# Second channel product with the weights stationary and 256 tokens moving, its results transposed in place

## The chip, the cores and the metric

The kernel runs on one core of a Trainium2 chip. The metric is device microseconds of one execution: three runs of the kernel before took 783.22, 783.54 and 783.66 us.

## The reference

Two blocks, all in float32. The first is a linear attention for 8 batches, 8 heads, 576 tokens and a head size of 64: `kv = k^T v` per head, `out = q kv`, divided by its root mean square over the head and multiplied by `g_norm`. Its result, as x with 8 x 576 rows of 512 columns, goes through an MLP mixer:

```
h  = relu(x^T w_tok1) w_tok2        # over the tokens: 576 -> 256 -> 576
u  = x + h^T
h2 = relu(u w_ch1) w_ch2            # over the columns: 512 -> 1536 -> 512
out = u + h2
```

The change concerns the last product, `relu(u w_ch1) w_ch2`, and how its result is added to u in `out`.

## The kernel before

**Stages.** Up to 188 us attention and token mixing run in four passes of two batches each, with the channel weights loaded beside them. Their order is written out by hand as lists of step names (`start`, `middle`, `steady`, `last`; lines 1242 to 1263 and 1302). The rows of u are written to `out` (the last 64 rows of each batch also to a tensor `u_rest`). The channel mixing then works on 9 "units" of 512 rows: the first 512 rows of each batch, and as ninth unit the 8 x 64 rows that are left. Unit 0 is a group of its own (`channel1_once`, `channel2_once`, 188 to 261 us); groups 1 to 4 are units (1, 2), (3, 4), (5, 6), (7, 8), each some 129 us: first channel product, then second.

**The products.** Each channel product is cut by Strassen's scheme twice: seven outer products `o`, each made of seven inner products `p`, so 49 per channel product and group. One inner product is one "place" in the order of the program: `products[place]` holds it, and `beside[place]` the steps of the other engines that are put behind it (`put`, line 858; they are issued place by place in the loop at line 1364). Products of neighbouring `o` overlap (`PLACE`, line 854): the last inner product of one stands at its place 9, behind the second of the next. An inner product of the first channel is 3 matmuls with 256 tokens moving (line 973); of the second, two halves of 128 tokens by 3 matmuls, with the activations stationary and 128 columns of weights moving (line 1028). Float32 matmuls are two records each in the trace. Results gather in three PSUM tiles `a`, `b` (one buffer each) and `d` (two). `outer` (line 861) moves them out: ScalarE copies some, VectorE adds others (`join`, line 921, at places 5 and 6 of an outer product), and a PSUM tile can only be used again after that. Into the second channel's results `r` (128 partitions by 4 x 256, tags `us` with three buffers and `r` with three) they go as rows of tokens.

**VectorE's own work beside it** are the sums that the inner products need as operands: `ins` (line 1080) for the second channel, `inner_u` for the first, with the sums of activations `S1` to `S4`, all at fixed places (lines 1106 to 1115). It also transposes the u of the next group in blocks of 32 x 32 (`turn_tile`, line 615), which SP sends to DRAM and fetches back (`put_blocks`, `fetch_half`).

**Weights and queues.** The parts of both weights lie in DRAM and are fetched for every outer product in four transfers, 12, 9, 7 and 4 places ahead (`fetch_ahead`, line 955), into two buffers each. SP issues nearly all transfers, in order. POOL issues the accumulating ones: `join` (line 1118) adds a finished `r` to the rows of u in `out`, one DMA of 128 x 4 x 1 KB per tile for units 1 to 7, two for unit 8. In the last group the half of the columns that is finished last isn't accumulated by DMA: u is loaded as `xg` (`fetch_x`, line 597), VectorE adds to it, and `store_rest` and `store_part` (lines 1163 and 1167) write it. The second weights are loaded by `get_ch2` (line 222), six blocks of 1 MB as pairs of 32-bit words, two DMAs each; `decode` turns them into float32 on ScalarE and VectorE. Parts of that weight's tile serve as scratch for early transposes of u (`turn_early`), so the decode of some blocks waits until SP's stores of these have landed.

Of the kernel before, what the change touches and what calls it, by code (L numbers as in the profile page):

```python
# [11 lines left out]
F32 = mybir.dt.float32  # L12
# [8 lines left out]
def kernel(  # L21
# [98 lines left out]
    def dma(o, i, engine=nc.sync):  # L120
        keep(engine.dma_start(o, i))
# [60 lines left out]
    def words(w):  # L182
        return w.bitcast(U32).rearrange("r (n w) -> r n w", w=2)
# [38 lines left out]
    def get_ch2(f):  # L222

        a = 2 * (2 * f // NS)

        def loads(raw):
            t = raw.rearrange("p (h f n) w -> p f h n w", h=2, f=2)
            rows = words(moe_w_ch2)[ts(f, 2 * P)].rearrange("(f p) (h n) w -> f p h n w", f=2, h=2)
            return [(t[:, i], rows[i]) for i in range(2)]

        dst = w_ch2[:, a:a + 2, ds(2 * f % NS, 2)]
        return block(2 * DM, loads, dst.rearrange("p h f n -> p h (f n)"))
# [357 lines left out]


    xg, xt, uT = {}, {}, {}

    def units(g):
        return (0,) if g == 0 else (2 * g - 1, 2 * g)

    def fetch_x(g, i):

        if g < NG:
            if i == 0:  # L600
                xg[g] = (late["xg"].tile([P, 2 * J, DH], F32, name="xg") if g else
                         late["xg0"].tile([P, J, DM], F32, name="xg"))
            rows = u_rows(units(g)[i])
            dma(xg[g][:, ts(i, J)], (rows[:, DH:] if g else rows).rearrange("(t p) e -> p t e", p=P))

    def fetch_t(u, i):

# [1 line left out]
            xt[u, i] = late["xt"].tile([P, DM], F32, name="xt")  # L609
            dma(xt[u, i], u_rows(u)[ts(i, P)])  # L610

    Q = 32
    blocks, blocks_dram = {}, {}

    def turn_tile(y, x, i):
# [181 lines left out]
    def channel2_once(g):  # L797

        shape = [P, 2, DH]
        x = xg[g]  # L800
        quarter = lambda i, j: x[:, 2 * i:2 * i + 2, ts(j, DH)]

        def product(n, ps, start, stop):
            for p in range(2):
# [19 lines left out]
        def seventh():  # L824
            product(7, p7, True, False)
            tensor_add(u3, p7, u2)
            tensor_add(quarter(0, 1), quarter(0, 1), u2)
            tensor_add(quarter(1, 0), quarter(1, 0), u2)

        def fifth():  # L830
            product(5, p5, True, False)
            tensor_add(u3, p5, u3)
            tensor_add(quarter(1, 1), quarter(1, 1), u3)

        def second():
            product(2, p1, False, True)
            tensor_add(quarter(0, 0), p1, quarter(0, 0))

        def fourth():
            product(4, p7, False, True)  # L840
            tensor_add(quarter(1, 0), p7, quarter(1, 0))
            store(1)

        def third():
            product(3, p5, False, True)
            tensor_add(quarter(0, 1), p5, quarter(0, 1))
            store(0)

        return [first, sixth, second, seventh, fifth, fourth, third]
# [11 lines left out]
    def outer(place, size, mul, to, base=None, act=copy, onto=False, last=False):  # L861

        banks, t = {}, {}
        places = LAST if last else PLACE
        w = size // P if size == T else W

        def fit(flat):
            return flat.rearrange("p (w t) -> p w t", w=w)

        def bank(name):  # L870
            banks[name] = late[name].tile([P, 2 * DM], F32, name=f"ps_{name}", tag=name)[:, :size]
# [148 lines left out]
    def channel2(g, n0):  # L1020
# [3 lines left out]
        def second(i, o):  # L1024
            n = n0 + i
            r = {}

            def mul(p, ps, start, stop):
                v = v_in_parts[g, o](p)
                w = w_part(n, p).rearrange("p (w e) -> p w e", w=W)  # L1030
                for t in range(2):
                    for s in range(W):
                        matmul(ps[:, ts(t, P)], lhsT=v[:, s, ts(t, P)], rhs=w[:, s],
                               start=(start and t == 0 and s == 0), stop=stop, skip_group_check=True)

            def to(i, j):
                if not r:
                    name = "us" if o in (1, 2, 6, 3) else "r"
                    r[0] = late[name].tile([P, J, DH], F32, name=name, tag=name)
                return r[0][:, ts(i, 2), ts(j, P)]  # L1040

            if g == NG - 1 and o == 3:
                outer(7 * n, T, mul, lambda i, j: xg[g][:, ts(i, 2), ts(j, P)], onto=True, last=True)
            else:
                outer(7 * n, T, mul, to, o == 6 and (lambda i, j: rs[1][0][:, ts(i, 2), ts(j, P)]))
            fetch_ahead(n)
            return r

# [50 lines left out]
            tensor_add(half(a21(), i), half(a21(), i), half(v_tile(g, 5), i))  # L1099

        radd = lambda o, a: do(lambda: tensor_add(rs[o][0], rs[o][0], rs[a][0]))
        xadd = lambda i, o: do(lambda: tensor_add(*2 * [xg[g][:, ts(i, J)]], rs[o][0]))
        A, S1, S2, S3, S4 = (halves(f) for f in (make_a21, sum1, sum2, sum3, sum4))


# [10 lines left out]
            put(b + place, *steps)  # L1116

        def join(i, j, o):
            u = units(g)[i]

            def add(to, a):
                keep(nc.gpsimd.dma_start(to.rearrange("t p e -> p t e"), a, accum_op=ALU.add))  # L1122

            def whole():
                add(out[u, :LO, ts(j, DH)].rearrange("(t p) e -> t p e", p=P), rs[o][0])

            def rest():
                for side in range(2):
                    add(out[side:B:2, LO:, ts(j, DH)], rs[o][0][ds(side * HF, HF)])

            return whole if u < B else rest

        def both(o, a, c):
            def step():
                rs[o] = {0: late["r"].tile([P, J, DH], F32, name="r", tag="r")}
                tensor_add(rs[o][0], rs[a][0], rs[c][0])

            return step

        for place, step in ((12, join(0, 0, 1)), (20, join(0, 0, 2)), (26, join(1, 0, 4)), (39, radd(7, 6)),  # L1140
                            (40, join(1, 0, 7))):
            put(b + place, step)
        if g < NG - 1:
            for place, step in ((46, both(57, 5, 7)), (46, join(1, 1, 57)), (47, radd(5, 6)), (52, radd(3, 5)),
                                (52, join(0, 1, 3))):
                put(b + place, step)
            if g == NG - 2:
                put(b + 60, do(fetch_x, g + 1, 0))
                put(b + 70, do(fetch_x, g + 1, 1))
        else:  # L1150
            for place, steps in ((38, [xadd(0, 6)]), (41, [xadd(1, 7)]), (44, [xadd(1, 5)]),
                                 (45, [store_rest]), (46, [xadd(0, 5)]),
                                 (48, [do(store_part, nc.scalar, 2, 4, P, DH), do(store_part, nc.sync, 0, 2, 0, DH)]),
                                 (49, [do(store_part, nc.sync, 2, 4, 0, P)])):
                put(b + place, *steps)

        for k, place in enumerate((6, 8, 12, 36)):
# [2 lines left out]
    def store(i):  # L1160
        dma(out[0, ds(2 * i * P, 2 * P)].rearrange("(t p) e -> p t e", p=P), xg[0][:, ts(i, 2)])

    def store_rest():
        for side, queue in enumerate((nc.scalar, nc.sync)):
            dma(out[side:B:2, LO:, DH:].rearrange("t p e -> p t e"), xg[NG - 1][ds(side * HF, HF), J:], queue)

    def store_part(queue, lo, hi, a, z):
        dma(out[B - 1, lo * P:hi * P, DH + a:DH + z].rearrange("(t p) e -> p t e", p=P),
            xg[NG - 1][:, lo:hi, a:z], queue)

    def weave(body, fill):
        done = 0
# [231 lines left out]
```

## Time and profile before

| | |
|---|---|
| median of three runs | 783.54 us |
| the profiled execution: its own time / its span | 783.41 / 781.6 us |
| attention, token mixing | 0 to 188 us |
| group 0 | 188 to about 261 us |
| TensorE matmuls busy | 769.3 us of the span |
| matmul, 128 columns moving (`ps_a<-w,v`) | 672 records, mean 275 ns |
| matmul, 256 columns moving (`ps_d<-ui,w`) | 504 records, mean 379 ns |
| accumulating DMA of 512 KB (`out_dram<-us`) | 11, median 7.8 us from issue to landing |
| weights (`w<-parts`, 384 KB) | 168, median 3.9 us from issue to landing |
| accumulating and plain stores from POOL (software queue) | 14656 packets, 22.02 MB, 13.7% of 16 engines |

A row of a group in this profile is: line, engine, operation, output and input by name, shapes, count; then busy us and the mean ns of one; then the engine's idle time just before and what ended it. Matmul records overlap, so their means are longer than the distance between two starts, and it is the distance that makes the time. PE is TensorE, PEld its weight loads, DVE is VectorE, ACT ScalarE, POOL GpSimd, SPq, ACTq and POOLq the engines' DMA issues.

### The profile page before, as it was taken

Reading aid. Unit: us, or ns where it says so; the run is one execution under the profiler, and the core shown is the slowest. Engines: PE = TensorE matmul, PEld = TensorE weight load, DVE = VectorE, ACT = ScalarE, POOL = GpSimd, SP = SyncE. Lnnn points to the kernel's source line nnn. Section 1 sums busy time; section 2 is a strip of 40 time slices with the busy share of each in tenths; the row PEclk is TensorE's granted clock in tenths of the full one; section 3 lists DMA queues with packets and bytes.
Section 4 is the critical chain, followed back from the end, with each engine's and each line's share of the span. In section 5 each row is a group of like instructions: output and inputs, shape, how many; then the busy total and the mean of one; then the engine's idle time right before and its main releaser. Section 6 shows DMA issues by size and latency. Waiting matters only on the chain.

```text
span 781.6 us, 14842 instructions
## 1 busy us (share of the span) xinstructions
PE 769.3 (98%) x5816; PEld 650.6 (83%) x5816; DVE 617.4 (79%) x924; ACT 271.1 (35%) x534; POOL 70.5 (9%) x84
## 2 busy tenths in 40 slices
PE   6999999999999999999999999999999999999998
PEld 5655555545888888999988899998889999889998
DVE  2867887897767779898768888876898885787977
ACT  2576565664210232511144241123352114325211
POOL 1002020113410000010100001010000101000111
PEclk9999999999999999999999999999999999999999
DMA  9999999599699795698996579889559889645864
GB/s 296 322 326 375 361 360 346 199 301 355 252 281 342 267 315 145 178 291 231 221 262 202 159 235 250 249 203 287 158 151 300 197 221 236 198 145 159 197 169 92
DMA packets 132613, 192.12 MB, mean 246 GB/s; under 512 B 13632, under 2 KB 92224, under 8 KB 132544
## 3 DMA queue, kind: packets, MB, share of 16 engines
q1 hardware_dynamic: 115984, 167.54, 68.1%
q0 software_dynamic: 14656, 22.02, 13.7%
q10 hardware_dynamic: 1904, 1.61, 0.7%
q8 instruction: 46, 0.75, 0.4%
q14 instruction: 23, 0.19, 0.1%
HBM read 138.31 MB, written 52.82 MB: 245 GB/s over the span
## 4 chain that ended last, share of the span: by engine, by line
PE 96%; DVE 1%; DMA 1%; ACT 1%; SPq 0%; issue 0%; ACTq 0%
PE ps_d L133 28%; PE ps_b L133 19%; PE ps_a L133 19%; PE ps_u L133 8%; PE ps_h L133 7%; PE ps_v L133 5%; PE ps_c L133 3%; PE ps_o L133 2%; PE ps_kv L133 2%; PE ps_w L133 2%; DMA raw<-in_moe_w_tok_dram 1%; DVE x L445 0%; PE ps_j L133 0%; DVE ms L466 0%; ACT x L499 0%; ACT sq L449 0%
## 5 line engine op out<-in xcount | busy, mean ns | idle before, releaser
L133 PE MATMUL ps_d<-ui,w 128*128 128x256 f32 x504 | 118.7, 379 | 0.0
L130 ACT COPY ps_d<-ps_a 128x768 f32<-128x768 f32 (+1 forms) x56 | 32.0, 571 | 215.3 <-PE ps_a L133 215.3
L133 PEld LDWEIGHTS ps_d<-ui,w 128*128 128x128 f32 x504 | 95.1, 190 | 12.9 <-DVE v L124 0.3
L124 DVE TENSOR_TENSOR v<-v,v 128x1536 f32<-128x1536 f32 (+2 forms) x70 | 103.4, 1482 | 0.3
L133 PE MATMUL ps_b<-w,sv 128*128 128x128 f32 x672 | 84.6, 276 | 0.0
L133 PE MATMUL ps_a<-w,v 128*128 128x128 f32 x672 | 84.2, 275 | 0.0
L133 PEld LDWEIGHTS ps_a<-w,v 128*128 128x128 f32 x672 | 79.8, 192 | 0.2
L133 PEld LDWEIGHTS ps_b<-w,sv 128*128 128x128 f32 x672 | 79.5, 192 | 0.2
L133 PE MATMUL ps_d<-w,v 128*128 128x128 f32 x528 | 66.2, 275 | 0.0
L133 PE MATMUL ps_h<-x,w_tok 128*128 128x512 f32 (+1 forms) x160 | 65.4, 603 | 0.6 <-DVE x L503 0.4
L133 PE MATMUL ps_u<-h,w_tok 128*128 128x512 f32 (+1 forms) x160 | 64.7, 599 | 0.0
L133 PEld LDWEIGHTS ps_d<-w,v 128*128 128x128 f32 x528 | 62.7, 192 | 0.3
L127 ACT ACTIVATE v<-v 128x768 f32<-128x768 f32 (+1 forms) x54 | 42.6, 821 | 55.1 <-DVE v L124 55.1
L133 PE MATMUL ps_d<-w,sv 128*128 128x128 f32 x480 | 60.1, 275 | 0.0
L133 PEld LDWEIGHTS ps_d<-w,sv 128*128 128x128 f32 x480 | 57.1, 192 | 0.2
L133 PEld LDWEIGHTS ps_h<-x,w_tok 128*128 128x128 f32 (+1 forms) x160 | 26.2, 189 | 32.3 <-issue 27.8
L133 PEld LDWEIGHTS ps_u<-h,w_tok 128*128 128x128 f32 (+1 forms) x160 | 25.6, 179 | 31.1 <-issue 26.7
L1122 POOL DMA_DIRECT2D out_dram<-us x11 | 14.2, 1292 | 379.5 <-ACT us L130 198.6
L133 PE MATMUL ps_a<-uT,w 128*128 128x256 f32 x192 | 46.7, 379 | 0.0
L133 PE MATMUL ps_b<-ui,w 128*128 128x256 f32 x168 | 40.8, 379 | 0.0
L133 PEld LDWEIGHTS ps_a<-uT,w 128*128 128x128 f32 x192 | 36.3, 190 | 4.8
L124 DVE TENSOR_TENSOR v<-ps_b,u 128x768 f32<-128x768 f32 x28 | 26.7, 954 | 15.3 <-PE ps_b L133 14.8
(145 smaller groups left out, 1207.0 us busy)
## 6 DMA issues: line engine op xcount, KB each, us to landing
w<-parts SPq DMA_DIRECT2D x168, 384.0 KB, 3.9
w<-parts SPq DMA_DIRECT2D x56, 192.0 KB, 3.3
uT<-blocks SPq DMA_DIRECT2D x36, 256.0 KB, 5.8
k_in<-in_k_dram SPq DMA_DIRECT2D x16, 512.0 KB, 8.9
qT<-in_q_dram SPq DMA_DIRECT2D x8, 1024.0 KB, 9.6
out_dram<-x POOLq DMA_DIRECT2D x16, 512.0 KB, 6.9
v_in<-in_v_dram SPq DMA_DIRECT2D x14, 512.0 KB, 9.2
raw<-in_moe_w_ch_dram SPq DMA_DIRECT2D x8, 768.0 KB, 8.7
```

The costliest lines, as they stand in the source:

```text
L124: keep(engine.tensor_tensor(out=o, in0=a, in1=b, op=op))
L127: keep(nc.scalar.activation(o, a, AF.Relu))
L130: keep(nc.scalar.copy(o, a))
L133: keep(nc.tensor.matmul(*a, **kw))
L1122: keep(nc.gpsimd.dma_start(to.rearrange("t p e -> p t e"), a, accum_op=ALU.add))
```

## The change

In the second channel product of groups 1 to 4 the weight part becomes the stationary operand and 256 tokens move: 3 matmuls per inner product and not 6. The result then has columns on the partitions. It is kept in a tile of 128 partitions by 16 blocks x 2 x 32, and VectorE transposes it in place, in blocks of 32 x 32 (`turn`), ahead of the DMA or store. So that a block becomes 32 tokens by 32 columns that belong together, the columns of the second weight are loaded in another order, in pieces of 256 bytes, eight DMAs per block; group 0, which shares these weights, adds its results with the order undone (`leaves`, two adds for one). After the transpose 32 partitions hold 64 columns of one token in 256 bytes, so an accumulating join becomes four DMAs (sixteen for unit 8). A tile can be transposed only when nothing more is to be added from it: the join of product 1 moves from place 12 to 38, that of product 7 from 40 to 51 (in group 4 it stays at 40), that of product 3 from 52 to 55. In the last group `xg` is loaded in 256-byte pieces, transposed in two steps in the first channel's stage so that results can be added to it, and transposed back in pieces ahead of the last stores, which are spread over the queues of SP, ACT and POOL.

```diff
@@ get_ch2
-            t = raw.rearrange("p (h f n) w -> p f h n w", h=2, f=2)
-            rows = words(moe_w_ch2)[ts(f, 2 * P)].rearrange("(f p) (h n) w -> f p h n w", f=2, h=2)
-            return [(t[:, i], rows[i]) for i in range(2)]
+            t = raw.rearrange("p (h f l b j) w -> p f l h b (j w)", h=2, f=2, l=2, b=NC)
+            rows = words(moe_w_ch2)[ts(f, 2 * P)].rearrange("(f p) (h b l j) w -> f l p h b (j w)", f=2, h=2, b=NC, l=2)
+            return [(t[:, i, l, h], rows[i, l, :, h]) for i in range(2) for l in range(2) for h in range(2)]
...
@@ channel2_once (group 0), at each of its adds to u
-            tensor_add(quarter(0, 0), p1, quarter(0, 0))
+            add_to(0, 0, p1)
...
@@ channel2
-                for t in range(2):
-                    for s in range(W):
-                        matmul(ps[:, ts(t, P)], lhsT=v[:, s, ts(t, P)], rhs=w[:, s],
-                               start=(start and t == 0 and s == 0), stop=stop, skip_group_check=True)
+                for s in range(W):
+                    matmul(ps, lhsT=w[:, s], rhs=v[:, s], start=(start and s == 0), stop=stop,
+                           skip_group_check=True)
...
-        for place, step in ((12, join(0, 0, 1)), (20, join(0, 0, 2)), (26, join(1, 0, 4)), (39, radd(7, 6)),
-                            (40, join(1, 0, 7))):
+        for place, step in ((20, join(0, 0, 2)), (26, join(1, 0, 4)), (38, join(0, 0, 1)), (39, radd(7, 6))):
             put(b + place, step)
         if g < NG - 1:
-            for place, step in ((46, both(57, 5, 7)), (46, join(1, 1, 57)), (47, radd(5, 6)), (52, radd(3, 5)),
-                                (52, join(0, 1, 3))):
+            for place, step in ((46, both(57, 5, 7)), (46, join(1, 1, 57)), (47, radd(5, 6)), (51, join(1, 0, 7)),
+                                (52, radd(3, 5)), (55, join(0, 1, 3))):
                 put(b + place, step)
             if g == NG - 2:
                 put(b + 60, do(fetch_x, g + 1, 0))
-                put(b + 70, do(fetch_x, g + 1, 1))
+                put(b + 70, do(turn, lambda: xg[g + 1][:, 0]), do(fetch_x, g + 1, 1))
+                put(b + 79, do(turn, lambda: xg[g + 1][:, 1]))
         else:
-            for place, steps in ((38, [xadd(0, 6)]), (41, [xadd(1, 7)]), (44, [xadd(1, 5)]),
+            for place, steps in ((38, [xadd(0, 6)]), (40, [xadd(1, 7), join(1, 0, 7)]), (44, [xadd(1, 5)]),
                                  (45, [store_rest]), (46, [xadd(0, 5)]),
-                                 (48, [do(store_part, nc.scalar, 2, 4, P, DH), do(store_part, nc.sync, 0, 2, 0, DH)]),
-                                 (49, [do(store_part, nc.sync, 2, 4, 0, P)])):
+                                 (48, [do(store_part, (nc.scalar, nc.sync), 1, (1,)),
+                                       do(store_part, (nc.gpsimd, nc.sync, nc.gpsimd, nc.scalar), 0, (0, 1))]),
+                                 (49, [do(store_part, (nc.sync, nc.scalar), 1, (0,))])):
                 put(b + place, *steps)
...
+    def turn(t):
+
+        t = t()
+        keep(nc.vector.transpose(t, t))
+
+    def pieces(u, j):
+
+        for b in range(NC):
+            cols = ds(j * DH + b * HF, HF)
+            if u < B:
+                yield b, slice(0, 2 * NQ), out[u, :LO, cols].rearrange("(n i) e -> i n e", i=Q)
+            else:
+                for side in range(2):
+                    for m in range(2):
+                        yield b, slice(2 * side + m, 2 * NQ, NC), out[side:B:2, ds(LO + m * Q, Q), cols].rearrange(
+                            "t i e -> i t e")
+
+    def put_rows(u, j, t, onto, queues=()):
+        turn(t)
+        for n, (b, at, to) in enumerate(pieces(u, j)):
+            a = t()[ds(b * Q, Q), at].rearrange("p n l j -> p n (l j)")
+            if onto:
+                keep(nc.gpsimd.dma_start(to, a, accum_op=ALU.add))
+            else:
+                dma(to, a, queues[n % len(queues)])
```

## Prediction

> **What bounds the kernel now.** I read the engines' totals and the chain of waits first, then the busy times by stage, then the timelines of the stages that the change touches.
>
> ```profile
> PE 769.3 (98%) x5816; PEld 650.6 (83%) x5816; DVE 617.4 (79%) x924; ACT 271.1 (35%) x534; POOL 70.5 (9%) x84
> ...
> PE 96%; DVE 1%; DMA 1%; ACT 1%; SPq 0%; issue 0%; ACTq 0%
> ```
>
> TensorE's matmuls are the end of nearly every step, so its time per product counts. The stages of group 2 (its first channel product, then its second), with busy us and counts by engine, then granted clock, DMA share and GB/s:
>
> ```profile
> 400.80:464.60 63.80, 63.80 (x344) 57.45 (x344) 51.33 (x72) 24.93 (x35) 0.00 (x0) 1.00 0.68 207
> 464.60:530.00 65.40, 65.40 (x542) 64.10 (x541) 55.10 (x71) 13.58 (x31) 7.73 (x6) 1.00 0.94 240
> ```
>
> TensorE never idles, at clock 1.00. VectorE has 10.3 us left in the second product's stage, and the DMA engines are 94% busy there against 68%. TensorE's timeline on both sides of the seam between the stages:
>
> ```profile
> 476.55 1.50 PE L133 MATMUL ps_a<-w,v 128*128 128x128 f32 x12
> 477.89 1.50 PE L133 MATMUL ps_b<-w,sv 128*128 128x128 f32 x12
> ...
> 523.45 1.46 PE L133 MATMUL ps_a<-uT,w 128*128 128x256 f32 x6
> 524.74 1.46 PE L133 MATMUL ps_b<-uT,w 128*128 128x256 f32 x6
> ```
>
> The starts matter, since the durations overlap. A second-channel product (12 records, 128 columns moving) takes 1.340 us, a first-channel one (6 records, 256 columns) 1.295.
>
> **Part 1, the products.** After the change every product of the groups has the second form: 0.045 us less on each of 4 x 49 = 196 products, 8.8 us at most. That is all TensorE can give, because even now a weight load is nearly hidden behind its matmul.
>
> **Part 2, the transposes.** VectorE's rows:
>
> ```profile
> L617 DVE STREAM_TRANSPOSE y<-xt 128x256 f32<-128x256 f32 x48 | 18.3, 419 | 3.6 <-DMA xt<-out_dram 3.6
> L124 DVE TENSOR_TENSOR r<-r,us 128x1024 f32<-128x1024 f32 x7 | 8.5, 1217 | 0.0
> ```
>
> A transpose of 256 elements takes what an add of 256 takes (413 to 425 ns), so I price one of 1024 as the add: 1.22 us, of which 1.14 passes before the next instruction starts. No row shows one in place. Below, it can't beat the one element per cycle of both rows; above, I allow twice, 2.4 us. Groups 1 to 3 get six each, 6.9 us into 10.3 us of idle time, of which TensorE's own gain takes 2.2. It matters where they fall. With "place" for one product's slot, VectorE's timeline from place 19 to 33 of group 2:
>
> ```profile
> 479.49 0.42 DVE L124 TENSOR_TENSOR r<-ps_b,u 128x256 f32<-128x256 f32 x1 [1.12 <-issue]
> ...
> 488.87 0.42 DVE L124 TENSOR_TENSOR r<-ps_b,u 128x256 f32<-128x256 f32 x1 [1.73 <-issue]
> 490.15 0.42 DVE L124 TENSOR_TENSOR r<-ps_d,p 128x256 f32<-128x256 f32 x1 [0.86 <-PE ps_d L133]
> ...
> 495.68 0.95 DVE L124 TENSOR_TENSOR sv<-v,sv 128x768 f32<-128x768 f32 x1
> ```
>
> The last makes the operand of place 33, whose weight load started at 496.68, 0.14 us late: already today VectorE is just in time there. TensorE would be there 32 x 0.045 = 1.44 us earlier, at 495.1. VectorE pays 1.14 at place 20 and 1.14 at place 26 and gets back the idle 1.12, 1.73 and 0.86; followed step by step it finishes the operand at 495.7. So TensorE now waits 0.64 instead of 0.14, 0.5 us lost in each of groups 1 to 3. Behind the transposes at 38, 46, 51 and 55 the adds that free a PSUM bank have 0.6 us left (place 43), 0.7 (place 51) and about -0.1 (place 58); I take 0.25 per group for these. In group 4, which prepares no next group, I find 0.2 lost up to the end of its place 37; what comes after is in part 5. Sum of parts 1 and 2: 3 x (2.2 - 0.75) + (1.7 - 0.2) = **5.9 us gained**.
>
> **Part 3, the accumulating DMAs** go from one of 512 packets of 1 KB to four of 512 of 256 B. In the packet records an accumulating packet of 1 KB takes 102 ns (median), a plain one 46, a plain 256 B one 18. If accumulating costs 2.2 times plain, 256 B takes 40 ns: per tile 2048 x 40 against 512 x 102, over 16 engines +1.9 us. Ends: 25 ns (a quarter of 102, no loss) and 102 (all per packet, +9.8 us a tile). I take 40, the rows of plain packets being nearest. Weight fetches start 12 places (15.5 us) ahead and land in 3.9, which covers it. The tile of product 1 is now sent at place 38, not 12, and product 3 writes the same buffer at place 46. From the end of place 37: transpose done at 3.35, four POOL issues of 1.28 until 8.6, landing about 4 later, 12.6; the copy must start by 13.7 or TensorE waits at place 49. So nothing; without that cover, up to 6 us in each of three groups.
>
> The Trainium skill speaks against this part. Its page "DMA: Bandwidth & Descriptors" (Specifications) puts the least transfer for line rate at 512 B, and (Why small descriptors are slow) 27% overhead on 256 B. The trace's four times 18 ns against one of 46 is 57%, more than that. By the page's figure a plain 256 B packet would be an estimated 14.6 ns, a block of part 4 would take 0.9 us less, and the sum would be at most that much lower, 784.6.
>
> **Part 4, loading the second weights.** Six blocks of 1 MB go from two DMAs each (2 KB packets, 84 ns) to eight (256 B): SP's issues rise from 1.2 to about 4.9 us per block (0.55 to 0.63 each), and 4096 x 18 against 512 x 84 adds 1.9 us of all 16 engines, which by the packet records were 80 to 111% busy from 158 to 190 us (packets counted where they start). Behind the fifth block SP sends eight block stores, and ACT waits for them:
>
> ```profile
> 168.22 1.17 ACT L163 ACTIVATE w_ch<-raw 128x1024 f32<-128x1024 f32 x1 [2.09 <-DMA blocks<-w_ch]
> ...
> 171.65 0.60 ACT L127 ACTIVATE h<-ps_h 128x512 f32<-128x512 f32 x1 [1.19 <-PE ps_h L133]
> ```
>
> The relu at 171.65 feeds the matmul at 172.40. Stores 2.3 to 3.7 us later put ACT's decode at 170.5 to 171.9, the relu 1.2 to 2.6 late, and TensorE 1.1 to 2.4. At 132.35 ACT waits for the first block too, but there TensorE has other work until 137.9. Against this, the SP queue may have slack I don't see. Ends: 0 and 5 us (all of SP's excess once). I take **1.4**.
>
> Group 0's split adds (six of 690 ns become twelve of 425) are 1 us of VectorE in a stage where it idles 10 of 46: nothing. The transposes and loads of group 4's x lie in a first-channel stage with 12 to 15 us idle: nothing.
>
> **Part 5, the end.** From the end of place 37 (761.9) to the end of the span is 19.7 us now. POOL's and VectorE's rows there:
>
> ```profile
> 77.99 0.58 POOL L121 DMA_DIRECT2D u_rest<-x  x1 [2.01 <-DVE x L124]
> ...
> 725.38 1.28 POOL L1122 DMA_DIRECT2D out_dram<-us  x1 [70.49 <-ACT us L130]
> ...
> 767.64 2.03 POOL L1122 DMA_DIRECT2D out_dram<-r  x2 [21.01 <-DVE r L124]
> ```
>
> VectorE after place 37, from 0.2 us on: a bank add 0.34, a sum 1.67, the transpose of product 1 (new, 1.14), two adds of 1.14, an operand 0.87, a bank add 0.34, an add 1.14 and the transpose of product 7 (new, 1.14), done at 9.1. The bank adds behind these come late, places 43, 44 and 49 start 0.5, 1.3 and 1.1 us late, and with the transpose of the rest (1.14) and three small ones (0.34, 0.6, 0.34) the last transpose ends at 19.4, where the last add ended at 16.9. Four small stores behind it, 13 issues of 0.35 to 0.45 on each of SP and ACT since 15.2, landing 2.0, 0.8 to close: 23.0 to 24.0. POOL is later still: from 9.2 it issues sixteen DMAs for product 7 where it had two. An issue of 128 descriptors is in no accumulating row; plain 128 took 0.58, accumulating 256 1.02. I take the middle, 0.80: until 22.0, then two stores of 0.74 queued behind them, landing 2.0, 0.8: 26.3. **Loss 6.6 us**; ends 3.3 (POOL at 0.58, then SP and ACT end last) and 8 (POOL at 0.9).
>
> **Sum**, against the profiled execution's 783.4 (span 781.6, and 1.8 around it; 0.1 below the shown median 783.54): 783.4 - 5.9 + 1.4 + 6.6 = **785.5**.
>
> **Rivals.** (a) *Faster*: POOL's small issues are cheap and SP's excess is hidden: 783.4 - 5.9 + 3.3 = 780.8. For it: the plain 128 at 0.58. It decides from about 0.6 us per issue and under 1 us at 172. (b) *The weight loads cost their upper end*: TensorE is held in the attention stage, 783.4 - 5.9 + 5 + 6.6 = 789.1. For it: DMA already full there; against: the prefetch is four buffers deep. (c) *VectorE becomes the bound*: an in-place transpose takes 2.4 us, and 1.2 more on 25 of them is 30 us, of which the idle time of the first-channel stages hides about a third: 785.5 + 20 = 805. Nothing but the lack of a row speaks for it. (d) *Small accumulating packets stay at 102 ns*: 3 x 6 us of waits for product 3's buffer and 8 more at the end: 783.4 - 5.9 + 1.4 + 6.6 + 26 = 811. Against: every other packet size gets cheaper. (e) *The change doesn't do what it says*: 256 tokens stream slower here than in the first channel product, whose shape is the same, and TensorE gains nothing: 783.4 + 1.4 + 6.6 = 791.4. I give it almost nothing.
>
> **How the numbers follow.** Forecast (782 to 787.5) 0.44, (a) 0.28, (b) 0.14, (c) 0.07, (d) 0.06, (e) 0.01. Faster and slower count from 0.2%, 1.6 us, about what measuring this kernel can tell. The forecast's own spread is half beyond 785.1 and half within, so same 0.23; (a) is all but 0.02 faster, 0.27 with a little of the forecast; slower 0.50. The range reaches from 779 (below (a), for an unstalled TensorE) to 794 (past (b) with its tail at 8) and leaves out (c) and (d).
>
> **What would show it.** Right: products 1.295 us apart in both stages; the load of place 33 waiting for VectorE by some 0.6 us; relu of the last pair at 173 to 174; POOL's issues for product 7 until after the last matmul, and a chain that ends POOL, DMA. Wrong: sixteen issues under 10 us in all; a 1024 transpose far from 1.22 us; gaps at place 49 behind ACT's copy, which would be (d); or TensorE waiting for weights.

## The result, and the profile after

The kernel after takes 791.73 us (median of four runs, 791.11 to 794.14; the kernel before beside it 783.60): a ratio of 1.0109, 95% interval 1.0097 to 1.0122, so 8.1 us slower. The forecast was 785.5 in a range of 779 to 794, with slower as the likeliest side. The side is right; of 8.1 us I had 2.1. The profiled execution took 792.06, its span is 790.3, 8.7 longer than before. One execution in the experiments, the profiled one of e10, ran at a granted clock of 0.851 and took 891.18 us; it is left out everywhere below. The engines' totals and the chain of waits:

```profile
PE 763.4 (97%) x4640; PEld 609.8 (77%) x4640; DVE 645.9 (82%) x958; ACT 271.1 (34%) x534; POOL 157.5 (20%) x174
...
PE 71%; DVE 10%; DMA 8%; POOL 4%; SPq 3%; issue 2%; ACT 2%; POOLq 0%; ACTq 0%; DVEq 0%
```

TensorE has 1176 records and 5.9 us of work less, and yet the chain, 96% TensorE before, now runs for 10% through VectorE, 8% through DMAs and 4% through POOL. VectorE has 28.5 us more work, POOL 87. The same two stretches of group 2 as in the prediction, busy us and counts by engine, clock, DMA share and GB/s. In both kernels they run from place 9 of one stage to place 9 of the next, some 12 us behind the seams between the stages (before: 388.9, 452.4 and 518.2 us), so that all six transposes of a group fall into the second:

```profile
400.50:465.35 64.85, 63.76 (x296) 55.81 (x295) 51.76 (x74) 24.97 (x36) 3.69 (x4) 1.00 0.77 210
465.35:529.50 64.15, 63.79 (x295) 55.55 (x294) 60.96 (x76) 13.52 (x31) 22.42 (x22) 1.00 1.09 236
```

The second stretch, mostly second-channel products, is 1.25 us shorter, as it should be. But the first, mostly first-channel products, which the change does not touch, is 1.05 longer, and TensorE idles there. In the second VectorE is down to 3.2 us idle and the DMA engines are full (packets are counted where they start, hence 1.09).

Step by step, after minus before, where minus is time gained. The stages overlap by a product or two at each seam, so every product, from its first matmul's start to that of the next product, is counted with the stage that it belongs to:

| stretch | us | forecast |
|---|---|---|
| attention to the start of group 1 | +1.05 | +1.4 |
| second-channel products of groups 1, 2, 3 | -1.52, -1.50, -1.51 | -1.45 each |
| group 4's, up to the end of place 37 | -1.43 | -1.5 |
| first-channel products of groups 1 to 4 | +0.1, +1.35, +2.0, 0.0 | 0 |
| from the end of place 37 to the end | +10.1 | +6.6 |

So two things are missing in the forecast: 3.5 us in the first-channel stages, and 3.5 more at the end.

**The first-channel stages.** What TensorE's weight loads waited for between 320 and 712 us, in total, times, and the longest:

```profile
PEld ps_d L133 <- DVE v L124: 3.6, 2, 2.1
PEld ps_b L133 <- DVE sv L124: 2.2, 3, 0.7
PEld ps_b L133 <- issue: 1.2, 3, 0.4
```

The kernel before has no such line in this stretch. The second line is place 33, 0.7 in each of three groups as forecast (0.64). The third is place 12, 0.4 in each, of which 0.2 delays the product itself; the profile names nothing that ended it, and it is gone in e9, where VectorE makes the operand of place 12 ahead of a sum. The first, 1.5 us at 410 and 2.1 at 540, was not in the forecast, and neither was the third. VectorE at the seam between groups 2 and 3, in lines of its timeline:

```profile
516.72 0.43 DVE L124 TENSOR_TENSOR us<-ps_b,u 128x256 f32<-128x256 f32 x1 [0.64 <-DMA out_dram<-us]
...
522.05 1.24 DVE L1165 STREAM_TRANSPOSE r<-r 128x1024 f32<-128x1024 f32 x1
...
526.67 1.24 DVE L1165 STREAM_TRANSPOSE us<-us 128x1024 f32<-128x1024 f32 x1
527.83 0.92 DVE L124 TENSOR_TENSOR v<-ps_d,p 128x768 f32<-128x768 f32 x1
528.67 0.75 DVE L623 STREAM_TRANSPOSE y<-xt 128x256 f32<-128x256 f32 x2
...
538.72 0.77 DVE L623 STREAM_TRANSPOSE y<-xt 128x256 f32<-128x256 f32 x2 [2.90 <-DMA xt<-out_dram]
539.41 0.92 DVE L124 TENSOR_TENSOR v<-ps_d,p 128x768 f32<-128x768 f32 x1
```

VectorE waits for `xt`, and the add behind it, at 539.41, frees the PSUM tile that TensorE needs next. Read upwards: the transposes of products 7 and 3 (522.05, 526.67) stand ahead of the one at 528.67 that frees an `xt` buffer, and before them VectorE waited 0.64 us (516.72) for the landing of product 1's join, whose buffer product 3 writes. The last two of these lines in the kernel before, without a wait:

```profile
536.25 0.76 DVE L617 STREAM_TRANSPOSE y<-xt 128x256 f32<-128x256 f32 x2
536.93 0.92 DVE L124 TENSOR_TENSOR v<-ps_d,p 128x768 f32<-128x768 f32 x1
```

SP's queue there, after and then before:

```profile
525.78 0.33 SPq L121 DMA_DIRECT2D xt<-out_dram  x1
526.20 0.41 SPq L121 DMA_DIRECT2D w<-parts  x1
529.45 2.84 SPq L121 DMA_DIRECT2D blocks<-y  x4
532.34 1.01 SPq L121 DMA_DIRECT2D xt<-out_dram  x1
```
```profile
529.20 1.78 SPq L121 DMA_DIRECT2D blocks<-y  x4
531.02 0.43 SPq L121 DMA_DIRECT2D xt<-out_dram  x1
```

The second fetch is issued at 532.34 and not 531.02, behind four block stores that SP now takes 2.84 us to issue, and it lands 6.4 us later where the slowest between 520 and 545 us took 5.0 before.

**The end.** POOL's timeline of the last 26 us, then SP's:

```profile
764.22 4.34 POOL L1184 DMA_DIRECT2D out_dram<-us  x4 [1.35 <-DVE us L1165]
770.33 14.23 POOL L1184 DMA_DIRECT2D out_dram<-r  x16 [1.78 <-ACT p L130]
781.11 4.67 POOL L121 DMA_DIRECT2D out_dram<-xg  x2
```
```profile
775.97 7.33 SPq L121 DMA_DIRECT2D out_dram<-xg  x13
```

The sixteen small DMAs of product 7 keep POOL busy from 770.33 to 784.56, the two stores queued behind them end at 785.78, and POOL's closing DRAIN, which in the kernel before ran from 768.1 to 774.3 beside other work, now runs from 781.6 to 789.5 and ends last, 3.7 us after the record of POOL's last DMA. The last product starts at 778.10 and the span ends 12.2 us later; before, it was 4.9.

The Trainium skill, "Perfetto Trace Analysis" (DMA Instruction — SWDGE (GPSIMD)), says that such a record on POOL ends when its descriptors are written, not when the data has moved. This trace agrees: the last record ends at 785.78, and packets of its queue ran until 786.9.

### The profile page after: what moved, and what is told of

The parts are those of the page before. It is cut to its first block, busy times and chain, and to the rows that moved or that the text cites. A ratio compares the mean times of both kernels' runs of the same rounds, so it can differ in the third digit from the quotient of the medians.

```text
span 790.3 us, 12750 instructions
## 1 busy us (share of the span) xinstructions
PE 763.4 (97%) x4640; PEld 609.8 (77%) x4640; DVE 645.9 (82%) x958; ACT 271.1 (34%) x534; POOL 157.5 (20%) x174
## 4 chain that ended last, share of the span: by engine, by line
PE 71%; DVE 10%; DMA 8%; POOL 4%; SPq 3%; issue 2%; ACT 2%; POOLq 0%; ACTq 0%; DVEq 0%
PE ps_d L133 20%; PE ps_b L133 14%; PE ps_a L133 14%; PE ps_u L133 6%; PE ps_v L133 5%; PE ps_h L133 4%; POOL out_dram L1184 3%; SPq L121 3%; PE ps_c L133 3%; DVE v L124 3%; DMA out_dram<-us 2%; PE ps_w L133 2%; PE ps_kv L133 2%; DMA xt<-out_dram 2%; PE ps_o L133 1%
## 5 line engine op out<-in xcount | busy, mean ns | idle before, releaser
L1184 POOL DMA_DIRECT2D out_dram<-us x44 | 47.9, 1723 | 403.6 <-ACT ps_d L130 364.7
L133 PE MATMUL ps_b<-sv,w 128*128 128x256 f32 x336 | 82.4, 381 | 1.4 <-DVE sv L124 1.0
L133 PE MATMUL ps_a<-v,w 128*128 128x256 f32 x336 | 81.7, 379 | 0.0
L1184 POOL DMA_DIRECT2D out_dram<-r x68 | 67.4, 2358 | 39.3 <-issue 23.2
L133 PEld LDWEIGHTS ps_b<-sv,w 128*128 128x128 f32 x336 | 63.2, 190 | 12.8 <-DVE sv L124 2.2
L133 PEld LDWEIGHTS ps_a<-v,w 128*128 128x128 f32 x336 | 63.8, 190 | 8.7
L133 PE MATMUL ps_d<-v,w 128*128 128x256 f32 x264 | 64.4, 380 | 2.4 <-DVE xg L124 1.2
L133 PE MATMUL ps_d<-sv,w 128*128 128x256 f32 x240 | 58.3, 379 | 0.0
L133 PEld LDWEIGHTS ps_d<-v,w 128*128 128x128 f32 x264 | 50.0, 190 | 9.9 <-DVE xg L124 1.6
L133 PEld LDWEIGHTS ps_d<-sv,w 128*128 128x128 f32 x240 | 45.6, 190 | 6.2
```

Source lines behind the costliest of these rows:

```text
L133: keep(nc.tensor.matmul(*a, **kw))
L1184: keep(nc.gpsimd.dma_start(to, a, accum_op=ALU.add))
```

## The experiments

Theory A: the small accumulating DMAs (their packets, and POOL's time for them) cause both losses. Theory B: the transposes make VectorE late at the seam, and this is what delays `xt`. At the end of the kernel I held POOL's sixteen DMAs to be the bound (A1). Times are medians; the kernel before ran beside each, at 783.3 to 783.6.

| run | us | ratio to before, 95% interval | TensorE's wait for the adds behind `xt` | last product's start to the end |
|---|---|---|---|---|
| after | 791.73 | 1.0109 (1.0097 to 1.0122) | 3.6 | 12.2 |
| e1 joins in 1 KB | 787.84 | 1.0046 (1.0030 to 1.0062) | 2.2 | 7.7 |
| e2 no transposes | 784.25 | 1.0008 (0.9997 to 1.0019) | none | 10.7 |
| e3 eight for sixteen | 789.16 | 1.0062 (1.0041 to 1.0084) | 4.1 | 9.0 |
| e4 POOL's stores moved | 793.76 | 1.0118 (1.0090 to 1.0145) | 4.3 | 11.4 |
| e5 `xt` turned later | 788.20 | 1.0056 (1.0037 to 1.0075) | none | 12.2 |
| e6 group 4 as before | 786.17 | 1.0037 (1.0015 to 1.0059) | 4.1 | 5.4 |
| e7 old weight loads | 791.46 | 1.0102 (1.0081 to 1.0122) | 3.8 | 12.2 |
| e8 joins moved too far | 831.65 | 1.0609 (1.0580 to 1.0638) | others | 5.2 |
| e9 order | 779.35 | 0.9944 (0.9930 to 0.9957) | none (1.9 at place 34) | 5.2 |
| e10 e5 and e6 | 780.73 | 0.9958 (0.9943 to 0.9973) | not used | not used |
| e11 eight and eight | 788.01 | 1.0064 (1.0041 to 1.0087) | 3.4 | 7.7 |
| e12 before, new loads | 784.20 | 1.0009 (0.9999 to 1.0020) | 2.2 in group 1 | 5.1 |

**e1, joins in packets of 1 KB**

```diff
@@ put_rows, accumulating
         turn(t)
+        if onto:
+            flat = t().rearrange("p n l j -> p (n l j)").rearrange("p (t e) -> p t e", e=DH)
+            if u < B:
+                keep(nc.gpsimd.dma_start(out[u, :LO, ts(j, DH)].rearrange("(t p) e -> p t e", p=P), flat,
+                                         accum_op=ALU.add))
...
+            return
```

> The kernel after, but every accumulating join is sent as before: one DMA of 512 packets of 1 KB per tile (two for unit 8), transposes kept. The rows that it adds to are then the wrong ones; every size and every step but the DMAs is that of the kernel after. Theory A (POOL's small DMAs and their packets cause both the wait for xt in the first-channel stages, 3.6 us, and the excess of the end): 781 to 783 us, no TensorE gap at 410 and 540, the end set by the stores of SP and ACT. Theory B (the transposes make VectorE late, and xt is late because VectorE frees its buffer late): the xt wait stays, only the end gains, 785 to 787.

Measured 787.84, above both ranges; in the profiled execution group 1 starts 1.1 us later than in the kernel after, which this edit doesn't touch. The gaps lie between the two theories: they shrink but stay.

```profile
PEld ps_d L133 <- DVE v L124: 2.2, 2, 1.4
```

So the small DMAs are a part of that wait, 1.4 us of 3.6, and not the whole of it. Here VectorE never waits for a join to land, and the `xt` fetch before the gap at 540 lands in 4.9 us and not 6.4. The end gains 4.5 (12.2 to 7.7), as both theories had it.

**e2, no transposes ahead of the joins**

```diff
@@ put_rows
-        turn(t)
+        if not onto:
+            turn(t)
```

> The kernel after without the transposes ahead of the accumulating joins (the last stores keep theirs), so what is added to the rows is not transposed; DMAs, places and packets stay. Theory B: place 33's wait (0.7 in three groups), place 12's and the xt waits (3.6) all go, with some 2 us of the end: 783 to 785. Theory A: place 33's and 12's waits go (3 us), the xt wait stays, and the end gains about 1.5, since POOL starts product 7 that much earlier: 786.5 to 788.

Measured 784.25, and of the first-channel waits nothing is left, with all the small packets still there:

```profile
PEld ps_b L133 <- DVE sv L124: 1.5, 3, 0.5
PEld ps_b L133 <- issue: 1.2, 3, 0.4
```

VectorE waits 0.7 us for `xt` where it waited 2.9, and TensorE does not wait for the adds behind it at all. That is theory B. Three things differ from what I wrote: place 12 keeps its 0.4; place 33 keeps 0.5 of its 0.7, since TensorE arrives earlier and VectorE has work enough without a transpose; and at the end the waits at places 43 and 44 go (2.3 us), the one at 49 (1.6) stays.

**e3, product 7 in eight DMAs of 256 descriptors**

```diff
@@ pieces, unit 8
-                for side in range(2):
-                    for m in range(2):
+                for m in range(2):
+                    if j == 0:
+                        yield b, slice(m, 2 * NQ, 2), out[:, ds(LO + m * Q, Q), cols].rearrange("t i e -> i t e")
+                        continue
+                    for side in range(2):
```

> The kernel after with product 7 of group 4 sent in 8 accumulating DMAs of 256 descriptors in place of 16 of 128 (both sides of the eight batches in one). Theory A1 (POOL pays per DMA, 0.88 us each of the sixteen, and its end, with the closing drain, is the end of the kernel): eight at 0.9 to 1.0 end 6 us earlier, and the stores of SP and ACT close instead: 785.5 to 787. Rival (POOL pays per descriptor): no gain, 791 to 792. Rival (the closing drain goes by the landing of the last store, not by POOL's own work): gain only what those land earlier, 788 to 790.

POOL's timeline:

```profile
769.55 7.62 POOL L1187 DMA_DIRECT2D out_dram<-r  x8 [1.79 <-ACT p L130]
778.84 1.20 POOL L121 DMA_DIRECT2D out_dram<-xg  x2 [1.67 <-DMA out_dram<-xg]
```

7.62 us where sixteen took 14.23: POOL pays per DMA, 0.95 each for 256 descriptors and 0.89 for 128. The two stores are now issued when their data is ready. From the last product to the end 9.0 us, 3.2 less; the median gains 2.6, less than the 5 to 6 I expected, because 13 issues on each of SP and ACT (until 783.2 and 783.9) come next. The median lies in the range of the second rival, but the trace speaks against it: POOL's DRAIN ends at 783.4, 3.3 us behind its own last record and 2.1 ahead of SP's (785.5).

**e11, both halves of unit 8 in eight** (e3's edit, for the plain stores of the rest too)

> The kernel after with both halves of unit 8 in 8 DMAs: the accumulating join of product 7 (as e3) and the plain stores of the rest on SP and ACT (8 in place of 16). If after e3 the end is that of the stores queued on SP and ACT, four issues less on each of them, 0.4 each: 1 to 1.7 us less than e3, from the last product's start to the end 7.3 to 8 us where e3 had 9.0 and the kernel after 12.2. Rival (it is the landing of the last transposed pieces, whatever is queued ahead): as e3.

SP's issues in the kernel e11:

```profile
776.44 6.56 SPq L121 DMA_DIRECT2D out_dram<-xg  x9
```

From the last product to the end 7.7, as expected, and 788.01 in all. So of the 7.3 us that the change adds behind the last product's start, 3.2 are POOL's sixteen DMAs, 1.3 four issues each on SP and ACT, and 2.8 are left, among them the transposes behind the last adds.

**e4, POOL's two last stores to SP and ACT**

```diff
-                                       do(store_part, (nc.gpsimd, nc.sync, nc.gpsimd, nc.scalar), 0, (0, 1))]),
+                                       do(store_part, (nc.scalar, nc.sync, nc.scalar, nc.sync), 0, (0, 1))]),
```

> The kernel after with the two last stores of POOL given to SP and ACT, one each; the sixteen DMAs of product 7 stay on POOL. If POOL's own sixteen are the bound, it saves only the two stores, 2 x 0.9 us less what SP and ACT get more: 789.5 to 790.5. If the stores queued behind them were the bound and the accumulating ones not, 786 to 787.

```profile
772.52 14.21 POOL L1184 DMA_DIRECT2D out_dram<-r  x16 [1.78 <-ACT p L130]
```

The sixteen take the same 14.2 us, then the DRAIN takes 4.2 more, and the stretch behind the last product shrinks by 0.8: the accumulating DMAs are the bound, not the stores. The median is 2.0 above that of the kernel after, not below as expected; in its profile the waits for `xt` are 0.7 longer and group 1 starts 1.5 later, neither of which this edit touches.

**e5, the third and fourth transpose of `xt` later**

```diff
-        for k, place in enumerate((3, 6, 9, 12, 50, 52, 67, 77)):
+        for k, place in enumerate((3, 6, 16, 20, 50, 52, 67, 77)):
```

> The kernel after, with the third and fourth transpose of the next group's u put at places 16 and 20 of a first-channel stage in place of 9 and 12; nothing else. Theory B (VectorE comes late into the stage, frees its xt buffer late, and the fetch queued behind it on SP lands late; TensorE pays only because the add that frees a PSUM bank stands behind that transpose): the gaps at 410 and 540 go and nothing takes their place before the next second-channel stage, 3.6 us less, 787.5 to 788.5. Rival (the VectorE backlog itself is the bound, the wait on the DMA only names it): new waits in the same stages, at most 1 us less, 790.5 to 792.

Measured 788.20, 3.5 less. What the weight loads waited for between 320 and 712:

```profile
PEld ps_b L133 <- DVE sv L124: 2.2, 3, 0.7
PEld ps_b L133 <- issue: 1.2, 3, 0.4
```

The line for `ps_d` is gone and nothing took its place: the transposed u belongs to the next group, and TensorE only paid because an add stood behind it in VectorE's order.

**e6, group 4 as before**

```diff
@@ channel2, group 4
+                if last:
+                    for t in range(2):
+                        for s in range(W):
+                            matmul(ps[:, ts(t, P)], lhsT=v[:, s, ts(t, P)], rhs=w[:, s],
+                                   start=(start and t == 0 and s == 0), stop=stop, skip_group_check=True)
+                    return
...
+        def at(x, i, j):
+            if last:
+                return x[:, ts(i, 2)].rearrange("p t (b l e) -> p t l b e", b=NC, l=2)[:, :, j]
...
-            return do(put_rows, units(g)[i], j, lambda: rs[o][0], True)
+            return do(put_whole if last else put_rows, units(g)[i], j, lambda: rs[o][0], True)
```

> Groups 1 to 3 as after; group 4 as before (activations stationary, 128 columns moving, no transposes, whole accumulating DMAs of 1 KB packets, joins of products 1 and 7 at 12 and 40), with the order of the columns undone by the engines' access patterns; the last 256 rows are stored whole. If the loss of the end belongs to group 4's part of the change alone, its second stage takes the 69.4 us of before and not 78.2: 782.5 to 783.5 us. Rival (the end is late because the stages ahead leave DMA queues or VectorE behind): 785 to 788.

In its profile group 4's second stage takes 69.9 us to the end, against 69.4 before and 78.2 after (all from the weight load of its second product): all but 0.5 of the loss belongs to group 4's part alone. POOL has two DMAs for product 7 again:

```profile
770.23 2.03 POOL L1202 DMA_DIRECT2D out_dram<-r  x2 [21.54 <-DVE r L124]
```

The median, 786.17, is higher than this gives (791.7 - 8.3 = 783.4): ten runs spread from 783.95 to 790.83. In the profiled one group 1 starts 2.0 us later than in the kernel after and the waits for `xt` are 0.5 longer. Why this kernel spreads more than the others stays open.

**e7 and e12, the loads of the second weights alone** (e7: after with the old loads; e12: before with the new ones; in both, the columns of the result are in another order)

```diff
@@ get_ch2, e7 (e12 is the reverse)
...
-            return [(t[:, i, l, h], rows[i, l, :, h]) for i in range(2) for l in range(2) for h in range(2)]
+            return [(t[:, i], rows[i]) for i in range(2)]
```

> The kernel after, with the second weights loaded as before, two DMAs of 2 KB packets per block, so that the columns of the result are in another order. My part 4 (1.4 us in the attention stage; 1.05 in the profiles shown, between executions whose first 46 us differ by as much): 0.5 to 1.5 us less than the kernel after, 790.2 to 791.2, no waits at 138 and 166 us. Rival (those waits come from how the execution starts and not from the loads): no difference, waits at 138 and 166 in this profile too.

> The kernel before with part 4 alone: the second weights in eight DMAs of 256 B pieces per block in place of two of 2 KB, so that the columns of the result are in another order; nothing else is changed. Part 4 as I priced it (1.4; the profiles with these loads reach the first channel product 142.3 to 144.7 us after the first kv matmul, those without 141.9 and 142.1): 784.3 to 785.0, ratio 1.001 to 1.002. Rival (the attention stage has slack enough, and e7's 0.3 is all): ratio 1.000 to 1.0005.

ScalarE in the kernel after, where part 4 is paid:

```profile
170.31 1.16 ACT L163 ACTIVATE w_ch<-raw 128x1024 f32<-128x1024 f32 x1 [2.04 <-DMA blocks<-w_ch]
...
172.70 0.60 ACT L127 ACTIVATE h<-ps_h 128x512 f32<-128x512 f32 x1 [0.17 <-PE ps_h L133]
173.56 1.09 ACT L127 ACTIVATE h<-ps_h 128x512 f32<-128x512 f32 x2 [0.26 <-PE ps_h L133]
```

The decode starts at 170.31 (168.22 before; forecast 170.5 to 171.9) and the first relu 1.05 later than the 171.65 of before (forecast 1.2 to 2.6). TensorE's matmuls wait in this stretch for ScalarE in the kernel after (0.5 us for `h`, 0.3 for `x`) and in e12 (1.5 and 0.3), and neither in the kernel before nor in e7. By the profiles the attention stage, counted from the kv matmul at 46 us, takes 142.1 (before) and 141.9 (e7) with the old loads, and 142.3 to 144.7 with the new ones, mean 143.5 over nine profiles: 1.5 us. By the medians it is 0.3 less in e7 and 0.8 more in e12, whose interval reaches from -0.1 to 1.6. Both agree with a price between 0.3 and 1.5; more precisely it can't be said.

**e8, a first attempt at a faster version**

```diff
-                (25, [ins[6][0]]), (29, [S4[0]]), (27, [ins[6][1]]), (28, [S1[1]]), (30, [ins[6][3]]),
+                (25, [ins[6][0]]), (34, [S4[0]]), (27, [ins[6][1]]), (28, [S1[1]]), (30, [ins[6][3]]),
...
-        for place, step in ((20, join(0, 0, 2)), (26, join(1, 0, 4)), (38, join(0, 0, 1)), (39, radd(7, 6))):
+        for place, step in ((20, join(0, 0, 2)), (26 if last else 41, join(1, 0, 4)), (12 if last else 38, join(0, 0, 1)),
+                            (39, radd(7, 6))):
...
-            for place, step in ((46, both(57, 5, 7)), (46, join(1, 1, 57)), (47, radd(5, 6)), (51, join(1, 0, 7)),
-                                (52, radd(3, 5)), (55, join(0, 1, 3))):
+            for place, step in ((46, both(57, 5, 7)), (47, radd(5, 6)), (58, join(1, 1, 57)), (60, radd(3, 5)),
+                                (61, join(1, 0, 7)), (65, join(0, 1, 3))):
```

> A version against both: e6's group 4; second weights in 2 KB packets, put in the new order by ScalarE while it decodes (halves of each block by two instructions); in groups 1 to 3 product 4 is transposed and joined at 41 and not 26, S4's first half is made at 34 and not 29, an operand of place 12 ahead of a sum, and products 5+7, 7 and 3 are transposed and joined at 58, 61, 65 in the next stage, where VectorE has idle time. If VectorE's order was what kept the gain, TensorE's 6.6 us of three groups come out almost whole: 776.5 to 778.5. Rival (VectorE has too much work for any order, or the moved joins meet the fetches of the next stage): 780 to 783.

Measured 831.65, far above both ranges. (It also makes half of S4 behind the step that overwrites its operand, so that sum is another one, of the same size.) Two waits, at the end of group 1's stage and in the first-channel stage behind it:

```profile
DVE r L124 <- DMA out_dram<-r: 8.6, 1, 8.6
PEld ps_b L133 <- DVE us L124: 6.2, 1, 6.2
```
```profile
DVE us L124 <- DMA out_dram<-us: 8.2, 1, 8.2
PEld ps_b L133 <- DVE v L124: 8.1, 1, 8.1
```

The sum of products 5 and 7 takes the buffer of product 4, whose join at 41 had not landed; a sum of the next u takes that of product 3. A join can be moved into idle time only as far as the landing of its DMA is ahead of the buffer's next writer.

**e9, the second attempt**

```diff
-        for k, place in enumerate((3, 6, 9, 12, 50, 52, 67, 77)):
+        for k, place in enumerate((3, 6, 16, 20, 50, 52, 67, 77)):
...
-                (8, [A[0]]), (9, [A[1]]), (10, [ins[2][3]]), (11, [S3[0]]), (12, [S3[1]]),
+                (8, [A[0]]), (9, [ins[2][3]]), (10, [A[1]]), (11, [S3[0]]), (12, [S3[1]]),
...
-                (25, [ins[6][0]]), (29, [S4[0]]), (27, [ins[6][1]]), (28, [S1[1]]), (30, [ins[6][3]]),
+                (25, [ins[6][0]]), (30, [S4[0]]), (27, [ins[6][1]]), (28, [S1[1]]), (29, [ins[6][3]]),
...
-            for place, step in ((46, both(57, 5, 7)), (46, join(1, 1, 57)), (47, radd(5, 6)), (51, join(1, 0, 7)),
-                                (52, radd(3, 5)), (55, join(0, 1, 3))):
+            for place, step in ((46, both(57, 5, 7)), (47, radd(5, 6)), (52, radd(3, 5)),
+                                (55, join(0, 1, 3)), (58, join(1, 1, 57)), (61, join(1, 0, 7))):
...
```

With it go e6's group 4 and a decode on ScalarE in two instructions for one, which put the columns in order.

> A second version against both kernels, with the lessons of e8's waits (product 4's join at 41 held the buffer that the sum at 46 needs, product 3's at 65 the one that the next stage needs): e6's group 4, e5's two transposes later, second weights in 2 KB packets put in order by ScalarE; in groups 1 to 3 one operand of place 33 ahead of S4's first half (29 and 30 changed round), one of place 12 ahead of a sum (9 and 10), and the joins in the order 3, 5+7, 7 at 55, 58, 61. Theory B (VectorE's order is what kept TensorE's gain): the waits at 12, 33, xt and at the end go, and 783.5 less 6.6 for three groups leaves 776.5 to 779. Rival (the 256 B packets keep the DMA engines too full in the next stage, and something else is late): 780 to 783.

779.35, just above the 776.5 to 779 of theory B and 0.56% faster than before (0.43 to 0.70); TensorE is busy for 98% of the span again. Between 320 and 712 us one wait is left, 0.6 in each of three groups, at place 34 now:

```profile
PEld ps_d L133 <- DVE v L124: 1.9, 3, 0.6
```

**e10, e5 and e6 together**

> e6 (group 4 as before) and e5 (two transposes later) together, nothing else moved, second weights in 256 B packets. If the two losses are separate, the sum of what each took off the kernel after: 791.7 - 8.8 - 3.6 = 779.3, by the measured medians 791.7 - 5.6 - 3.5 = 782.6; so 779 to 783, and the gaps at places 12 and 33 (0.3 and 0.65) and at 138 and 166 us are left.

780.73, within the range: the two losses are separate, and 11.0 us come back. e9 is 1.4 faster still, by its order and its loads together; what each gives wasn't tried by itself (e9's attention stage takes 142.6, within the spread of the others).

## Why the prediction was right and wrong

- **Bound and part 1, right.** The prediction's two windows are not the stages that it calls them: they start some 12 us late. Cut at the seams, VectorE's idle time in the second-channel stage of group 2 was 11.1 us before, not 10.3, and is 5.4 after; the argument stands. In the second channel's stage two products now start 1.29 us apart, as in the first's, by TensorE's timeline in the kernel after:

```profile
480.90 1.46 PE L133 MATMUL ps_a<-v,w 128*128 128x256 f32 x6
482.19 1.46 PE L133 MATMUL ps_b<-sv,w 128*128 128x256 f32 x6
```

  Parts 1 and 2 together gave 6.0 us (1.52 + 1.50 + 1.51 + 1.43), forecast 5.9.
- **Part 2, right in size, incomplete in reach.** The transposes take 1.235 us (forecast 1.22), place 33 waits 0.7 (0.64). That the sum fits to a tenth is partly luck: the 0.25 a group that I took for places 43, 51 and 58 was lost at none of them in groups 1 to 3, and 0.2 was lost at place 12, which I had not looked at. But "Behind the transposes at 38, 46, 51 and 55 the adds that free a PSUM bank have 0.6 us left" counts bank adds up to place 58 and stops there. VectorE carried its lateness into the next stage, where a transpose of `xt` frees a buffer that SP is waiting to fill.
- **Part 3, the step that failed first.** "Weight fetches start 12 places (15.5 us) ahead and land in 3.9, which covers it" holds for weights: TensorE never waited for them. It left out the `xt` fetches, which start when VectorE frees their buffer and are needed six places later. Price 3.6 us of waits, 3.5 in the table; VectorE's lateness and its order are the cause (e2 and e5: all of it goes), the small DMAs make it worse (e1: 1.4 of it goes). The sign stood in the prediction's own row of L617: in group 1 of the kernel before VectorE already waited 2.6 and 1.0 us for `xt`, and TensorE 0.3 behind the second, at 280 us; in e12, which has no transpose of results at all, these are 2.7, 2.8 and 2.2. An accumulating packet of 256 B takes 46 ns (median; forecast 40), so rival (d) is out. The buffer of product 1 came free 13.2 us behind the end of place 37 (forecast 12.6); TensorE waited for it nowhere, VectorE 0.64 us in groups 1 and 2.
- **Part 4, right.** 1.4 forecast; 0.3 to 1.5 measured.
- **"The transposes and loads of group 4's x lie in a first-channel stage with 12 to 15 us idle: nothing."** Right: that stage shows no wait (0.0 against before).
- **Part 5, right mechanism, mis-sized: 6.6 forecast, 10.1 measured.** In its own terms, from the end of place 37: POOL starts at 9.9 and not 9.2 (0.7); its sixteen take 14.2 and not 12.8 (1.4); the stores behind them 1.2 and not 1.5 (-0.3); and "landing 2.0" was 3.7 for POOL's DRAIN (1.7). The prediction took the same 2.0 for POOL's queue as for SP's and ACT's small stores. The upper end, 8, had POOL's price right (0.9 for one issue, 0.89 measured) and was too low for the start and this landing. If POOL's excess goes, SP and ACT are next, as the lower end had it (e3, e11).
- **Rivals.** (a) is out: an issue of 128 descriptors costs 0.89 and not under 0.6. (c) and (e) are out by the durations above. (b) is out: the loads cost 0.3 to 1.5, not 5. The sum of (e), 791.4, is the one nearest to the 791.7 measured, by chance: its condition is refuted by the 1.29 us above.

So 785.5 and 791.7 differ by 3.5 (the `xt` wait that I had not looked for) and 3.5 (POOL's end), less 0.1 in parts 1 and 2 and 0.35 in part 4: 6.55, against 8.7 - 2.1 = 6.6 in the profiled execution. That 791.7 lies in the range is partly luck: its upper end was set past rival (b), the weight loads, and these cost little.

## What to carry to other kernels

Work added to an engine that is almost full is not only paid where it stands but also at later places where that engine frees a buffer: follow the delay across the seam until the idle time that absorbs it, and ask of every buffer on the way which fetch it holds up. A DMA split into pieces costs its issuing engine by the piece, and where those are the last of the kernel, nothing hides them; here one group in the old form at the end, and two transposes moved to where their result is soon enough, made the same change 0.4% faster than the kernel before (e10) instead of 1.1% slower.

## What the runs showed of the hardware

- POOL's time for an accumulating DMA of 256-byte pieces hardly depends on the number of descriptors: 0.89 us for 128 (14.23 / 16), 0.95 for 256 (7.62 / 8), 1.09 for 512 (4.34 / 4). A line through these is some 0.82 us per DMA and 0.5 ns per descriptor, an estimate.
- POOL's closing DRAIN ends 2.8 to 4.9 us after the record of its last DMA (e1 2.8, after 3.7, e4 4.2, before 4.6, e9 4.9), and where it ends last (after, e2, e4) 0.8 us go to the end of the span. By these numbers a last DMA of POOL whose record ends 6 us ahead of the end costs nothing there, as in the kernel before (769.7 of 781.6).
- An accumulating packet takes 102 ns for 1 KB and 46 ns for 256 B (medians), a plain one 46 and 18: the small ones cost 1.80 and 1.57 times as much per byte.
- Executions differ by more than 1 us before the kv matmul at 46 us (it starts at 45.8 to 47.2 in these profiles) and by 2.4 in the attention stage with the same loads (142.3 to 144.7); the kernel before took 782.7 to 786.1 us over all its executions. Gains of 1 us were read from the stage, not from the medians.
